# The last two blocks of a four-layer attention kernel cut into parts, under a newly written order of all work

## The chip, the cores and the metric

The kernel runs on one core of a Trainium2 chip. The metric is the device time in microseconds (us) of one execution. The kernel before was timed six times: 332.86 to 335.13 us, median 334.13 us. One more execution was profiled; it took 333.49 us, and its span from the first to the last instruction is 331.8 us. TensorE is called PE here, VectorE DVE, ScalarE ACT, GpSimd POOL; SP is the engine whose queue issues most transfers.

## The reference

x has 2048 tokens of width 512, in bf16. Four layers follow each other, A B A B, each with a residual; both have 32 heads of 16.

```
def _A_ref(x, wqkv, w_phi, wo):                    # linear attention
    q, k, v = split(x @ wqkv)                      # per head
    pq = einsum("bhsd,hdf->bhsf", q, w_phi);  pk likewise
    phi_q = concat([softmax(pq), softmax(-pq)]);  phi_k likewise
    kv = einsum("bhsf,bhsd->bhfd", phi_k, v);  z = einsum("bhsf->bhf", phi_k)
    o = einsum("bhqf,bhfd->bhqd", phi_q, kv) / (einsum("bhqf,bhf->bhq", phi_q, z) + 1e-6)
    return merge_heads(o) @ wo

def _B_ref(x, wqkv, wo):                           # window of 8 keys, 2 apart
    q, k, v = split(x @ wqkv)
    idx = pos[:, None] - 2 * arange(8)
    logits = where(idx >= 0, q . k[idx] / 4, -1e9)
    return merge_heads(softmax(logits) . v[idx]) @ wo

x = x + _A_ref(_layernorm(x), ...)
x = x + _B_ref(_layernorm(x), ...)     # and both once more
```

## The kernel before, in words

The tokens are cut into four blocks of 512, each of four tiles of 128 tokens; x stays in SBUF, as x0 to x3. A stage of the model is one Python function, called for layer pair L (0 or 1) and block b (0 to 3). A function does not issue its work: it puts small steps on named threads, one thread for each stage and engine (`step`). `run` then walks a long written table, `_ORDER`, whose words each name a thread, and issues that thread's next step. Since every engine works through its own instructions in the order in which they were issued, this one table sets the order on PE, DVE, ACT and SP alike. Three more tables belong to it. `_CHOICE` has one digit for each flexible step (`flex`): whether a copy out of PSUM, a normalisation or a residual goes to DVE or to ACT. `_SLOTS` says which buffer each tile takes, in four pools: "big" (8 buffers: the key exponentials Ek, the replicated values Vg, the products prod and pav), "med" (16), "t2" (6) and "ps" (the 8 PSUM banks). A tile that takes a buffer waits until the readers of the one before it are done.

The stages that the change and the prediction speak of:

- Loads (`s_loads`): x0 in four tiles of 128 KB, the raw query and key weights (wraw), the value weights (WA), x1 to x3 in 512 KB each, all on SP's queue. The weights are folded with w_phi on PE before the first projection.
- `s_a1`, keys and values of an A layer: L575 makes the keys of a tile, L581 their exponentials (ACT, +k and -k), L587 the values. On DVE four adds that halve each time (L608 to L621) give the softmax sums, ACT turns them into reciprocals by logarithm and exponential (rr), and L633 multiplies the exponentials of the whole block, 4096 elements a partition. L650 sums keys times values over all tokens, 16 small matmuls a tile, into one PSUM bank for the layer (kvp): nothing that needs the state can start before the last block's L633 and L650.
- `s_a2`: L680 makes queries, L688 their exponentials Eq, L696 (indS) the sums.
- `s_akv`, the change-over from keys to queries: the state is copied (kvT), transposed (L726), and spread into the zero-padded ZM (L735) and R (L739) on DVE.
- `s_a3`: L764 makes the denominators with ZM, DVE and ACT make rho from them. For blocks 0 and 1 PE spreads rho over the heads' rows (L790, bc, into four banks) and DVE multiplies Eq by it from PSUM, tile by tile (L796, mulp). For blocks 2 and 3 rho goes through DRAM instead (Prho, L814). `s_a4` multiplies by the state (L855), and copies oT out of PSUM.
- `s_b1`: the projections of a B layer (L879), copied to QT, K and V. K and V carry 16 tokens of the block before at their front: K's halo is copied on DVE (L905), V's on ACT in two steps (L917, L921, by way of vh). `vrep` then writes V in 32 transfers a block, each 32 partitions high and shifted, into Vg (L931, SP).
- `s_b2`: prod (L960, DVE) multiplies queries by the shifted keys, 4096 elements a partition, one for each of four c; L967 sums over the head (lgt); ACT makes exponentials, PE and ACT the reciprocal sum, DVE the weights PT (L995).
- `s_b3`: pav (L1020, DVE) multiplies PT by Vg, 4096 elements, one for each of four q; L1027 (mo) sums into PSUM, and a copy puts the result into oT.
- `s_out`: for each of four tiles `mm` makes four products that add up over c (L511), one for each q of oT, then the residual: either PE adds x by an identity matmul (L514, "onpe") and ACT copies the result out (L521), or DVE adds x from SBUF (L524). After the last layer two tiles at a time are stored (L535, SP, 256 KB).
- `s_flag`: three small DVE operations count whether the fast path's number ranges were kept, PE sums them over the partitions, three more DVE operations decide. Every engine loads the outcome into a register at the end (L1072) and branches to a general path, which does not run here.

In the last 30 us of the order before, the last four stages of blocks 2 and 3 run beside each other. DVE has the last prod, two pav, PT, six pav in a row, the three counts, a residual of x3, the three deciding operations, three residuals of x3 and three of x2. PE has four sums, the sixteen output products of block 3, the last two sums of block 2 together, and then the sixteen output products of block 2.

## Time and profile before

| | us |
|---|---|
| median of six runs | 334.13 |
| the profiled execution | 333.49 |
| its span | 331.8 |
| PE busy | 311.5 |
| DVE busy | 300.4 |
| ACT busy | 281.4 |
| POOL busy | 5.8 |

Busy time counts an engine's instructions without idle time; matmuls are pipelined and their ends are modelled, so PE's figure says that PE had work, not that it was at its peak. Streams of 512-column matmuls follow each other at 0.22 us (0.86 us for four), although each is shown with 380 ns. The transfers of Vg land 4.8 us after their issue (median), the stores of 256 KB 4.1 us, the first loads of x (128 KB) 4.2 us. POOL has 32 instructions in all, and nearly all of them fill a tile with a constant. The granted clock of PE is full until some 310 us, and 0.83 to 0.87 after that.

### The profile page before, as it was taken

To read this page: it belongs to the slowest core of one execution; us is meant where nothing else is said; L and a number is where in the kernel's file an instruction comes from. 1 tells how busy PE (TensorE), PEld (TensorE's weight loads), DVE (VectorE), ACT (ScalarE), POOL (GpSimd) and SP (SyncE) were. 2 spreads that over 40 slices of the span, in tenths; PEclk is the share of its full clock that TensorE was granted. 3 is DMA by queue.
4 is the path that set the end of the run, shared out by engine and by line. 5 is a ranking of instruction groups with operands and counts; after the bars stand their busy time and mean duration, and the time that the engine had idled before them with its cause. 6 is when DMAs were issued, how large, how long until landed. Compare 5 with 4: busy or idle time off the path is not lost.

```text
span 331.8 us, 7975 instructions
## 1 busy us (share of the span) xinstructions
PE 311.5 (94%) x3189; PEld 149.9 (45%) x3189; DVE 300.4 (91%) x422; ACT 281.4 (85%) x644; POOL 5.8 (2%) x32
## 2 busy tenths in 40 slices
PE   8999997999999999999999999789999999997792
PEld 4545446445444444443444455534444444443231
DVE  5899995898899899999999999498999999999983
ACT  4999995999998898999999999688899997685630
POOL 4000000000000000000000000000000000000000
PEclk9999999999999999999999999999999999999988
DMA  7980000014499889785990200022469988789905
GB/s 208 330 226 3 0 0 4 4 35 103 97 158 140 154 136 164 128 136 117 143 129 14 54 0 2 6 56 90 115 109 144 126 155 174 131 142 155 209 5 168
DMA packets 37325, 35.42 MB, mean 107 GB/s; under 512 B 22944, under 2 KB 32160, under 8 KB 37280
## 3 DMA queue, kind: packets, MB, share of 16 engines
q1 hardware_dynamic: 36752, 34.81, 55.6%
q8 instruction: 27, 0.44, 0.6%
q14 instruction: 18, 0.15, 0.2%
q10 hardware_dynamic: 528, 0.02, 0.1%
HBM read 10.50 MB, written 2.36 MB: 39 GB/s over the span
## 4 chain that ended last, share of the span: by engine, by line
PE 65%; DVE 13%; ACT 11%; DMA 5%; issue 3%; SPq 1%; DVEq 0%; ACTq 0%
PE ps L879 19%; PE ps L511 13%; PE ps L575 6%; PE ps L587 6%; PE ps L680 5%; DMA xnT<-xn 4%; PE ps L967 3%; DVE Eq L796 3%; PE ps L1027 3%; DVE prod L960 3%; ACT oT L186 2%; DVE Ek L633 2%; ACT sqd L531 2%; PE ps L453 2%; PE ps L650 2%
## 5 line engine op out<-in xcount | busy, mean ns | idle before, releaser
L879 PE MATMUL ps<-xnT,WB 128*128 128x512 bf16 x384 | 88.5, 380 | 1.0 <-ACT V L186 0.7
L960 DVE TENSOR_TENSOR prod<-QT,K 128x4096 bf16<-128x4096 bf16 x32 | 72.2, 2287 | 1.1 <-ACT K L186 0.9
L1020 DVE TENSOR_TENSOR pav<-PT,Vg 128x4096 bf16<-128x4096 bf16 x32 | 71.7, 2287 | 0.9 <-PE ps L967 0.4
L879 PEld LDWEIGHTS <-WB 128*128 128x128 bf16 x384 | 42.2, 115 | 44.7 <-issue 7.4
L511 PEld LDWEIGHTS <-oT 128*128 128x128 bf16 x256 | 24.1, 99 | 32.9 <-ACT oT L186 4.0
L186 ACT CAST oT<-ps 128x512 bf16<-128x512 f32 x57 | 31.4, 603 | 7.7 <-PE ps L1027 6.6
L688 ACT ACTIVATE Eq<-ps 128x512 bf16<-128x512 f32 x64 | 35.0, 613 | 1.2 <-PE ps L680 1.1
L581 ACT ACTIVATE Ek<-ps 128x512 bf16<-128x512 f32 x64 | 34.2, 626 | 0.0
L511 PE MATMUL ps<-WoA,oT 128*128 128x512 bf16 x128 | 31.2, 380 | 1.4 <-ACT oT L186 1.4
L511 PE MATMUL ps<-WoB,oT 128*128 128x512 bf16 x128 | 32.5, 389 | 0.0
L680 PE MATMUL ps<-xnT,WA 128*128 128x512 bf16 x128 | 31.0, 380 | 1.0 <-issue 0.8
L587 PE MATMUL ps<-WA,xnT 128*128 128x512 bf16 x128 | 30.7, 379 | 0.0
L575 PE MATMUL ps<-WA,xnT 128*128 128x512 bf16 x128 | 30.0, 379 | 0.4 <-DMA xnT<-xn 0.4
L531 ACT ACTIVATE sqd<-x 128x512 bf16<-128x512 bf16 x48 | 30.0, 635 | 0.3
L524 DVE SCALAR_TENSOR_TENSOR x<-ps,x 128x512 bf16<-128x512 f32 x36 | 23.5, 685 | 1.0 <-PE ps L511 0.8
L521 ACT ACTIVATE x<-ps 128x512 bf16<-128x512 f32 x28 | 16.5, 598 | 8.0 <-PE ps L514 7.6
L439 ACT ACTIVATE xn<-x,nmr,rstd 128x512 bf16<-128x512 bf16 x27 | 21.4, 822 | 2.0 <-DVE nmr L428 2.0
L186 ACT CAST QT<-ps 128x512 bf16<-128x512 f32 x30 | 17.3, 593 | 3.6 <-issue 2.5
L796 DVE TENSOR_TENSOR Eq<-ps,Eq 128x512 bf16<-128x512 f32 x32 | 19.7, 681 | 0.1
L1027 PE MATMUL ps<-pav,indAV 128*32 128x512 bf16 x256 | 17.4, 389 | 2.6 <-DVE pav L1020 2.6
L186 ACT CAST K<-ps 128x512 bf16<-128x512 f32 x30 | 17.7, 596 | 2.1 <-PE ps L879 1.8
L186 ACT CAST V<-ps 128x512 bf16<-128x512 f32 x31 | 17.5, 602 | 2.3 <-PE ps L879 2.3
(126 smaller groups left out, 405.7 us busy)
## 6 DMA issues: line engine op xcount, KB each, us to landing
Vg<-V SPq DMA_DIRECT2D x128, 131.5 KB, 4.8
Prho<-rd SPq DMA_DIRECT2D x8, 512.0 KB
out_dram<-x SPq DMA_DIRECT2D x8, 256.0 KB, 4.1
x<-in_A_x_dram SPq DMA_DIRECT2D x3, 512.0 KB, 6.6
WB<-in_B_wqkv_dram SPq DMA_DIRECT2D x3, 512.0 KB, 11.5
wraw<-in_A_wqkv_dram SPq DMA_DIRECT2D x4, 256.0 KB
x<-in_A_x_dram SPq DMA_DIRECT2D x4, 128.0 KB, 4.2
WA<-in_A_wqkv_dram SPq DMA_DIRECT2D x1, 512.0 KB
```

Source lines behind the costliest of these rows:

```text
L186: self.nc.scalar.copy(out=out, in_=in_)
L511: nc.tensor.matmul(y[:], lhsT=oT[:, c, t * P:(t + 1) * P], rhs=Wo()[:, c, :], start=(c == 0), stop=(c == NB - 1 and not onpe))
L531: nc.scalar.activation(out=sqd[:], in_=xb[:, t, :], func=ACT.Square, accum_out=T["ss"][:, t:t + 1])
L575: nc.tensor.matmul(pk[:], lhsT=xnT[:, t, k, :], rhs=self.WA[:, k, D:2 * D], start=(k == 0), stop=(k == NB - 1))
L581: nc.scalar.activation(out=T["E"][:, t, s, :], in_=T["k", t][:], func=ACT.Exp, scale=1.0 - 2.0 * s)
L587: nc.tensor.matmul(pv[:], lhsT=xnT[:, t, k, :], rhs=self.WA[:, k, 2 * D:3 * D], start=(k == 0), stop=(k == NB - 1))
L680: nc.tensor.matmul(pq[:], lhsT=self.WA[:, k, hb * P:(hb + 1) * P], rhs=xnT[:, :, k, :], start=(k == 0), stop=(k == NB - 1))
L688: nc.scalar.activation(out=self.Eq[L, b][s][:, :, hb, :], in_=T[hb][:].rearrange("p (t i) -> p t i", t=4), func=ACT.Exp, scale=1.0 - 2.0 * s)
L796: nc.vector.tensor_tensor(out=ev, in0=T["pb", s][t][:].rearrange("p (a i) -> p a i", a=NB), in1=ev, op=ALU.mult)
L879: nc.tensor.matmul(pp[:], lhsT=self.WB[:, k, i * D + c:(i + 1) * D:NB], rhs=xnT[:, :, k, :], start=(k == 0), stop=(k == NB - 1))
L960: nc.vector.tensor_tensor(out=pr[:], in0=QT[:, c:c + 1, :].to_broadcast([P, NW, TB]), in1=win, op=ALU.mult)
L1020: nc.vector.tensor_tensor(out=pv[:], in0=PT[:].unsqueeze(1).to_broadcast([P, NB, 2, TB]), in1=vw, op=ALU.mult)
```

## The change

The three tables `_ORDER`, `_CHOICE` and `_SLOTS` are written anew throughout, so every engine's order differs from the first tenth of the work on. Besides:

- For blocks 2 and 3 of the last layer (`split`) the output product of a tile comes in two steps: three of the four products (q = 0, 1, 2) on a thread of their own, which may be issued early, and the fourth with the residual. The last pav, its sums and its copy are cut into two halves of 256 tokens. Each tile is stored for itself.
- In `s_a3` each multiplication by rho is flexible: ACT first copies the PSUM bank to SBUF (bs) and DVE multiplies from there, or DVE reads PSUM as before.
- The key sums of block 3 go in two halves of two tiles in both A layers (`half_k`).
- The halo copies of K and V run on POOL, and POOL's order is now set by the table too.
- The register loads of the flag are issued 12 words of the table after its deciding step, not at the very end (`flag_lag`); on SP this puts the load ahead of the last store. On the other engines it stays last.

```diff
-    "half_k": (),
+    "half_k": ((0, 3), (1, 3)),
+    "split": ((1, 2), (1, 3)),
+    "flag_lag": 12,
...
-_ORDERED = {_E.PE, _E.DVE, _E.Activation, _E.SP}
+_ORDERED = {_E.PE, _E.DVE, _E.Activation, _E.SP, _E.Pool}
...
-        def mm(t, onpe):
+        def mm(t, onpe, cs=range(NB)):
             oT = self.oT[key, b]
-            T[t] = y = self.ps()
-            for c in range(NB):
+            if cs[0] == 0:
+                T[t] = self.ps()
+            y = T[t]
+            for c in cs:
                 nc.tensor.matmul(y[:], lhsT=oT[:, c, t * P:(t + 1) * P], rhs=Wo()[:, c, :],
                                  start=(c == 0), stop=(c == NB - 1 and not onpe))
-            if onpe:
+            if onpe and cs[-1] == NB - 1:
...
+        split = last and (1, b) in _OPT["split"]
+        if split:
+            for t in range(4):
+                add(st + "p", "PE", mm, t, False, range(NB - 1))
         for t in range(4):
-            add(st, "PE", mm, t, _CHOICE[self.nflex] == "1")
+            if split:
+                add(st, "PE", mm, t, _CHOICE[self.nflex] == "1", range(NB - 1, NB))
...
+            elif last and split:
+                add(st, "SP", store, t, t + 1)
...
+        def bev(s, t, direct):
+            if direct:
+                self.slot("t2")
+            else:
+                T["bs", s, t] = self.t2([TB], "bs")
+                nc.scalar.copy(out=T["bs", s, t][:], in_=T["pb", s][t][:])
...
-            nc.vector.tensor_copy(out=self.K[L, b][:, :, 0:16], in_=self.K[L, b - 1][:, :, TB:KVW])
+            nc.gpsimd.tensor_copy(out=self.K[L, b][:, :, 0:16], in_=self.K[L, b - 1][:, :, TB:KVW])
...
-            nc.scalar.copy(out=T["V"][:, :, 0:16], in_=self.vh[L, b - 1][:])
+            nc.gpsimd.tensor_copy(out=T["V"][:, :, 0:16], in_=self.vh[L, b - 1][:])
...
-            nc.scalar.copy(out=self.vh[L, b][:], in_=T["V"][:, :, TB:KVW])
+            nc.gpsimd.tensor_copy(out=self.vh[L, b][:], in_=T["V"][:, :, TB:KVW])
...
         for q in range(NB):
-            add(st, "DVE", pav, q)
-            add(st, "PE", mo, q)
-            self.flex(st, ev, q)
+            m = 2 if q == NB - 1 and (L, b) in _OPT["split"] else 1
+            for i in range(m):
+                a = (i * TB // m, TB // m)
+                add(st, "DVE", pav, q, *a)
+                add(st, "PE", mo, q, *a)
+                self.flex(st, ev, q, *a)
```

How the instructions of the two kernels stand against each other, counted over the whole program:

| instruction | before | after |
|---|---|---|
| DVE, Eq times rho from PSUM / from SBUF | 32 / 0 | 21 / 11 |
| ACT, rho from PSUM to SBUF (bs) | 0 | 11 |
| DVE, residual with sums / of the last layer | 29 / 7 | 34 / 4 |
| PE, identity product of a residual (and its ACT copy) | 28 | 26 |
| xn on DVE / on ACT | 37 / 27 | 44 / 20 |
| DVE, copies of oT, of the rest (QT, K, V, WA, kvT, vaug) | 7, 16 | 11, 12 |
| halo copies on DVE / ACT / POOL | 6 / 12 / 0 | 0 / 0 / 18 |
| L633 over 4096 / over 2048 elements | 8 / 0 | 6 / 4 |
| pav over 4096 / over 8 x 256 | 32 / 0 | 30 / 4 |
| output stores of 256 KB / of 128 KB | 8 / 0 | 4 / 8 |

The order at the places that matter here. At the start SP issues all four tiles of x0 before the first weights (three before, and the fourth later), and the value weights after x1 to x3 (after x1 in before); DVE makes the mask constants before its first statistics, and PE's first projections are twelve query products and sixteen key products, then values (in before keys, then values). At the change-over of each layer the last L650 that waits for DVE has 32 matmuls (64 or 80 in one piece in before); query products stand between the last L650, the transposes and the denominators in the first layer, and the 32 indS products of one block in the second. In the tail DVE has the last prod, two pav, PT, and then block 3's four pav (the last in halves) and block 2's last three (the last in halves), the counts, two residuals of x2, the deciding operations and two more. Block 3's four residuals are on PE and ACT. PE's output products of blocks 3 and 2 stand in pieces of three to six between the sums; the fourth tile of each block has its four products together, after the last half of the sums. On SP a store of two tiles of block 1, which waits for ACT, stands between the fourth and fifth of the last eight Vg loads.

## The prediction

> **What bounds the kernel now.** First the page: busy shares, then busy time by stretch, to see which engine has room in which stage.
>
> ```profile
> PE 311.5 (94%) x3189; PEld 149.9 (45%) x3189; DVE 300.4 (91%) x422; ACT 281.4 (85%) x644; POOL 5.8 (2%) x32
> ```
>
> ```profile
> 89.20:178.20 89.00, 88.16 (x604) 38.98 (x606) 86.77 (x84) 83.88 (x201) 1.31 (x4) 1.00 0.85 135
> 178.20:211.30 33.10, 32.08 (x481) 17.48 (x477) 28.67 (x49) 30.97 (x69) 0.00 (x0) 1.00 0.09 18
> 211.30:319.70 108.40, 100.44 (x980) 45.96 (x976) 104.67 (x117) 86.00 (x205) 0.15 (x1) 0.98 0.70 124
> 319.70:331.80 12.10, 6.18 (x40) 2.25 (x38) 5.03 (x15) 1.67 (x3) 0.00 (x0) 0.87 0.34 115
> ```
>
> The columns after the length are busy PE, weight loads, DVE, ACT, POOL, clock, DMA. In the first B layer (89 to 178) DVE is idle 2.2 us of 89.0, in the second (211 to 320) 3.7 of 108.4: DVE work added there is paid almost in full. Between them, at the change-over from keys to queries, PE and ACT are the full ones. The last 12.1 us hold little of anything. Next the waits of DVE in the second half, and the chain that ended last:
>
> ```profile
> DVE ZM L735 <- PE ps L726: 3.3, 1, 3.3
> ```
>
> ```profile
> 312.96 2.29 DVE pav L1020
> 315.25 0.04 issue
> 315.30 1.05 PE ps L1027 x7
> 316.34 4.62 PE ps L511 x16
> 320.96 0.98 PE ps L1027 x16
> 322.05 2.75 PE ps L511 x12
> 325.02 0.88 PE ps L511 x4
> 325.92 0.69 DVE x L524
> ```
>
> One change-over wait costs DVE 3.3 us in one piece. In the tail the last value product (pav) begins at 317.4 and ends at T = 319.65; its sums (L1027) start only at 320.89, behind sixteen output products of the other block; all sixteen products of the last block follow; the last residual ends at 326.61, so 6.96 us after T. The store is issued then and the span ends at 331.8, 5.2 us later. Prices, from the groups by line:
>
> ```profile
> L796 DVE TENSOR_TENSOR Eq<-ps,Eq 128x512 bf16<-128x512 f32 x32 | 19.7, 681 | 0.1
> L616 DVE TENSOR_TENSOR s<-s 128x512 bf16<-128x512 bf16 x8 | 3.4, 424 | 0.2
> L596 POOL MEMSET vaug<- 128x64 bf16 x8 | 2.8, 486 | 112.4 <-PE ps L511 64.0 <-PE ps L680 45.3 <-DVE prod L960 3.0
> L905 DVE COPY K<-K 128x64 bf16<-128x64 bf16 x6 | 1.1, 176 | 0.0
> L909 POOL MEMSET K<- 128x64 bf16 x2 | 0.3, 152 | 26.6 <-PE ps L855 26.6
> ```
>
> **What the Trainium skill says.** "VectorE: DVE Perf Modes", section The perf-mode tier table: a tensor-tensor operation on bf16 in SBUF runs at 2x, one with a PSUM operand at 1x. The trace agrees: 681 ns from PSUM, 424 ns for the same 512 elements from SBUF. "SBUF — State Buffer", section Who interferes with whom: a DVE instruction with two SBUF inputs contends with a GpSimd instruction that reads SBUF, and whichever starts first holds the ports for its whole length. Nothing here shows it: POOL only fills tiles during the work of before, and the change gives it 18 copies that read. "DMA: Bandwidth & Descriptors", section Anatomy of one DMA: most of a small transfer is a fixed cost, the wait for the write's receipt. The trace agrees: stores of 256 KB land in 3.8 to 4.3 us, loads of 128 KB in 4.2 (median).
>
> **The change, part by part.** The sum is made against the profiled execution (span 331.8, its own time 333.49; the median of the six runs is 334.13, 0.6 above it).
>
> Tail. The last pav comes in halves, and three quarters of most tiles' output product need only the three earlier q. After T, DVE has: three flag counts (0.28 past T in before), two residual tiles at a 0.62 pitch (L524), the three deciding instructions (322.09 to 322.63, 0.54), and two more residuals, 0.62 + 0.69. That is 3.4 us. PE's side runs beside it: eight half-width sums (about 0.5 with latency), one half cast (about 0.4; the full one is 0.60), then a last product and the four fused ones of the last tile (0.87 + 0.2), residual 0.69: some 3.1. I take 3.7, with 0.3 for waits between engines. Gain 6.96 - 3.7 = 3.3. Bounds: 2 (the clock at 0.87 and PE late) to 4. The last store is 128 KB instead of 256: nothing. SP's load of the flag (492 ns, after the last store in before) now stands ahead of the last store; the flag is ready two residuals before that store's data, 1.3 us, so it is hidden; without that cover it costs 0.5.
>
> A store moved in SP's queue: the first half of block 1 is stored between the fourth and fifth of the last eight Vg loads. It waits for two ACT residuals of block 1. From the pav before the last PT: 0.5 (sums) + 1.15 (two casts) + 2.3 (eight products, two identities) + 0.6 is 4.6 us, then 0.42 for the issue, 2.9 for four loads at 0.73, 4.8 to land: 12.7. The split pav that reads them stands 0.6 + 6 x 2.2 = 13.8 behind the same point. Hidden with 1.1 to spare; if landing takes 6.8 it costs 0.9.
>
> DVE work up to T. Eleven of 32 rho products read an SBUF copy: 11 x 0.257 = -2.8. Six K halos go to POOL: -1.1. Five more residuals with sums, 0.70 each from start to start: +3.5. Seven more xn at 0.33 (three take 1.06): +2.3. One more xnT copy: +0.6. The other casts from PSUM change places but not number. Halves of the last key block in both layers: each of five instructions costs about 0.15 more, less what overlaps: +1.2. Halved pav: +0.15. Sum +3.8; with the overlap of neighbours counted along the two instruction lists I get +3.3. By place: about +1 before the first change-over, +1.6 in the first B layer, -0.5 from there to the second change-over, +1.4 after it. ACT: 11 copies at 0.60 (+6.6), 12 halo copies (-3.1), seven xn (-5.5), two residuals and five accumulator reads (-2.2), the rest about +0.4: some -4 in all, so the copies fit into ACT, idle 22 us from 211 to 320. PE: two identity products fewer, -0.4.
>
> Change-overs. Second: in before, from the end of the last Ek product (208.0) to the zero-padded states (ZM, 211.29) DVE waits 3.3: 64 kv products (1.1), cast 0.6, a 0.95 stop of the PE queue at the indS products ahead of the transposes. With halves only 32 kv follow the last product (0.55), and the indS products stand complete beside the cast: 0.6 + 0.6 + 0.4 + 0.15 = 1.8, a gain of 1.5. First: the last Ek product ends at 51.7 and ZM comes at 56.34, with 1.8 us of DVE work in the gap that now lies elsewhere (the mask constants in the wait for x at the start). The like sum gives 2.0. DVE alone would reach ZM 2.6 earlier; PE has 1.2 less to stream up to the last kv; ACT has some 2 us more before the last Ek, mostly filler. I take 1.6. Against it the start: the fourth tile of x is now issued ahead of the weights on SP, 0.43 to 0.50 for its issue, and PE waits for these weights from 5.94: +0.4. Net 1.2. Bounds 0 to 2.6. Loading the value weights behind all of x lets them land some 3 us later, but the value products now come after twelve query and sixteen key products (28 x 0.22 = 6 us): covered.
>
> POOL copies. Lower bound nothing (each runs while DVE waits or reads PSUM); upper bound 0.49 each, as the strided memset, held against DVE: 18 x 0.49 = 8.8. A plain 64-element memset takes 0.15. I take nothing and keep the upper end as a rival.
>
> Sum: -3.3 (tail) - 1.2 (first change-over and start) - 1.5 (second) + 1.6 - 0.5 + 1.4 (DVE work) = -3.5. From 333.49 that is 330.0; from the median 330.6. I say 330.2.
>
> **The rivals.** A, larger gain: the new order also removes waits in the middle. DVE is idle 5.1 us between 56.3 and 89.2 and the first change-over could give 2.6. Half of the former and all of the latter: -3.5 - 2.5 - 1.4 = -7.4, 326.1. For it: DVE is not the full engine there. Against: PE is busy 31.9 of 32.9 us in that stretch. B, the tail alone: ACT, 98% busy from 20 to 40 us, makes the first change-over no earlier, and the second is eaten by the 1.9 us of DVE work ahead of it: -3.5 + 2.7 = -0.8, 332.7. For it: ACT's and PE's fill there. C, slower: POOL's reading copies take the shared port between two DVE instructions, and the next prod or pav waits. At 0.39 us, the median memset of vaug, all 18 cost 7.0: -3.5 + 7.0, so 337.0. It decides from (3.5 + 1.7) / 18 = 0.29 us a copy. For it: the B layers have DVE back to back, so no copy finds the port free for long. Against: a small copy may be nearer to 0.15, and where DVE waits anyway it costs nothing.
>
> **How the numbers follow.** Half a per cent, 1.7 us, is about what a measurement of this kernel can tell from no change: faster is below 332.5, slower above 335.8. Forecast 0.48 (327.5 to 332.5), A 0.20, B 0.17, C 0.15. Faster: nearly all of the forecast's, all of A, four tenths of B, some 0.72; same 0.13; slower 0.15. The range goes from 325.5 (A with a little more) to 334.8 and leaves out C and the end of A.
>
> **What would show it.** From the end of the last pav half to the last residual 3 to 4 us, and to the end of the span some 9 instead of 12.15. The wait of ZM for the transposes below 2 us in the second layer. DVE busy 301 to 302 in all. Rho products from SBUF at 0.42. POOL copies at 0.15 to 0.25, and prod and pav still at 2.29 without holes before them. Wrong if prod or pav last 2.5 or more, or start late, beside POOL copies (C); if DVE waits for Vg before the last pav halves (the moved store); or if ZM is not earlier than 56.3 and 211.3 (B).

## The result, and the profile after

The changed kernel takes 332.79 us (median of 34 runs, 330.5 to 334.4), the kernel before 334.23 us (71 runs, 332.4 to 336.93). The ratio is 0.9945, 95% interval 0.993 to 0.996. So 1.4 us by the medians, 1.8 by the ratio, where 3.9 were forecast (334.13 to 330.2): the sign is right, the size more than twice too large. The profiled execution took 332.49 us, its span is 330.7.

The page's first row after, to be read against the row of before:

```profile
PE 310.8 (94%) x3203; PEld 149.5 (45%) x3203; DVE 302.5 (91%) x443; ACT 279.5 (85%) x634; POOL 26.8 (8%) x50
```

DVE has gained 2.1 us and ACT lost 1.9. The prediction's list of instructions had +3.3 to +3.8 for DVE and some -4 for ACT: the directions are right, the sizes about half. POOL stands at 26.8 instead of 5.8, for 18 more instructions.

The same execution by stage. The columns after the length are busy PE, weight loads, DVE, ACT, POOL, clock, DMA share and GB/s; the cuts are the first ZM, the first prod, the last pav of the first B layer, ZM of the second layer, the last pav (T in the prediction), the last residual, the end.

```profile
0.00:54.40 54.40, 51.80 (x593) 28.54 (x594) 48.38 (x105) 46.98 (x98) 5.19 (x30) 1.00 0.43 117
54.40:86.69 32.29, 31.59 (x503) 15.67 (x502) 27.45 (x68) 31.21 (x75) 0.15 (x1) 1.00 0.17 44
86.69:179.61 92.92, 90.54 (x652) 40.77 (x650) 88.91 (x88) 84.18 (x199) 7.95 (x10) 1.00 0.78 132
179.61:210.94 31.33, 30.90 (x457) 16.58 (x457) 28.17 (x50) 29.58 (x67) 0.00 (x0) 1.00 0.10 19
210.94:321.25 110.31, 102.79 (x982) 46.76 (x983) 106.28 (x125) 86.91 (x199) 13.53 (x9) 1.00 0.68 121
321.25:325.14 3.89, 3.17 (x22) 1.18 (x20) 3.28 (x12) 0.61 (x2) 0.00 (x0) 1.00 0.72 252
325.14:330.70 5.56, 0.00 (x0) 0.00 (x0) 0.01 (x1) 0.00 (x0) 0.00 (x0) 0.83 0.29 83
```

Before, the same cuts lie at 56.34, 89.18, 178.25, 211.29, 319.65, 326.61 and 331.80. The first prod comes 2.5 us earlier; the last pav of the first B layer 1.4 later; the second ZM 0.35 earlier; T, which was to be slightly earlier, 1.6 later; then the end wins. So in this pair of executions the gain of the first change-over is given back in the next 93 us, and that of the second change-over in the 110 us after it.

The waits of DVE from 205 us to the end of the last pav (total, times, longest), which answer to the 3.3 us shown of before:

```profile
DVE ZM L749 <- PE ps L740: 1.8, 1, 1.8
DVE x L529 <- PE ps L516: 1.3, 2, 1.0
```

1.8 is the very figure that the prediction worked out for the second change-over. And the tail, in the chain of waits:

```profile
319.19 1.10 ACT oT L189 x2
320.29 0.05 issue
320.34 0.39 PE ps L516
320.73 0.33 PE ps L1045 x8
321.06 1.18 PE ps L516 x5
322.25 0.01 PE ps L1079
322.25 0.33 PE ps L1045 x8
322.58 1.85 PE ps L516 x8
324.43 0.02 issue
324.45 0.69 DVE x L529
```

Where before sixteen output products (L511, here L516) kept PE from the sums of the last pav until 1.2 us after T, eight half-width sums now run at 320.7, the other half's at 322.25, and only eight products remain behind them. From T to the last residual 3.89 us, forecast 3.7: DVE's own list is as long as was forecast, and it waits once, 0.46 us, for PE. Yet the last residual ends at 325.14 against 326.61: 1.5 us, not 3.3.

**One execution or several.** Two more profiles of the kernel before were taken (e11 and e15), and three experiments below leave nearly everything up to T as it is (e2 puts the last pieces together again, e4 moves only the flag's load, e9 one load of Vg). So each stretch is known from three executions of the old order and four of the new:

| stretch, us | before | after | difference of means | forecast |
|---|---|---|---|---|
| start to first prod | 89.2, 90.7, 89.8 | 86.7, 86.4, 86.2, 86.1 | -3.5 | |
| first prod to last pav, layer 0 | 89.1, 89.2, 89.2 | 92.9, 92.6, 94.0, 93.7 | +4.2 | |
| the two together | 178.3, 179.9, 178.9 | 179.6, 179.0, 180.2, 179.8 | +0.6 | +0.4 |
| to second ZM | 33.0, 32.8, 32.8 | 31.3 (all four) | -1.5 | -2.0 |
| to the last pav | 108.4, 108.3, 108.3 | 110.3, 110.2, 110.1, 110.2 | +1.9 | +1.4 |
| to the last residual | 7.0, 5.6, 5.6 | 3.9 (without e2) | -2.2, or -1.7 without the 7.0 | -3.3 |
| to the end | 5.2, 5.4, 5.0 | 5.5, 5.5 (changed kernel, e9) | +0.3 | 0 |

Without the 7.0 the differences add up to -0.4 us, with it to -0.9: less than the measured 1.4 to 1.8. Spans of single executions scatter by 1 us; the clock, under e11 and e15 below, accounts for most of the rest. The largest difference from the forecast is the tail.

### The profile page after: what moved, and what is told of

Same layout as the page of the kernel before. It is cut to its first block, busy times and chain, and to the rows that moved or that the text cites. A ratio compares the mean times of both kernels' runs of the same rounds, so it can differ in the third digit from the quotient of the medians.

```text
span 330.7 us, 8061 instructions
## 1 busy us (share of the span) xinstructions
PE 310.8 (94%) x3203; PEld 149.5 (45%) x3203; DVE 302.5 (91%) x443; ACT 279.5 (85%) x634; POOL 26.8 (8%) x50
## 4 chain that ended last, share of the span: by engine, by line
PE 62%; ACT 13%; DMA 11%; DVE 8%; SPq 3%; issue 2%; ACTq 0%; DVEq 0%
PE ps L893 19%; PE ps L516 10%; DMA Vg<-V 7%; PE ps L601 6%; PE ps L589 6%; PE ps L694 5%; PE ps L981 3%; ACT Ek L595 3%; ACT Eq L702 3%; DMA xnT<-xn 3%; PE ps L1045 2%; SPq L945 2%; DVE Eq L812 2%; PE ps L456 2%; ACT sqd L536 2%
## 5 line engine op out<-in xcount | busy, mean ns | idle before, releaser
L1036 DVE TENSOR_TENSOR pav<-PT,Vg 128x4096 bf16<-128x4096 bf16 (+1 forms) x34 | 71.8, 2163 | 1.9 <-DMA Vg<-V 1.2
L516 PEld LDWEIGHTS <-oT 128*128 128x128 bf16 x256 | 23.6, 98 | 34.4 <-ACT oT L189 4.3
L189 ACT CAST oT<-ps 128x512 bf16<-128x512 f32 (+1 forms) x55 | 29.5, 584 | 8.1 <-PE ps L1045 7.7
L516 PE MATMUL ps<-WoB,oT 128*128 128x512 bf16 x128 | 32.8, 380 | 0.3
L516 PE MATMUL ps<-WoA,oT 128*128 128x512 bf16 x128 | 30.9, 380 | 1.6 <-DVE x L529 1.4
L694 PE MATMUL ps<-xnT,WA 128*128 128x512 bf16 x128 | 31.3, 380 | 0.2 <-DVE Eq L812 0.2
L529 DVE SCALAR_TENSOR_TENSOR x<-ps,x 128x512 bf16<-128x512 f32 x38 | 24.9, 685 | 2.2 <-PE ps L516 2.1
L189 ACT CAST K<-ps 128x512 bf16<-128x512 f32 x32 | 18.7, 590 | 3.6 <-PE ps L893 3.5
L1045 PE MATMUL ps<-pav,indAV 128*32 128x512 bf16 (+1 forms) x272 | 17.6, 370 | 3.3 <-DVE pav L1036 2.9
L935 POOL COPY vh<-V 128x64 bf16<-128x64 bf16 x6 | 7.4, 1234 | 161.9 <-ACT V L189 161.9
L526 ACT ACTIVATE x<-ps 128x512 bf16<-128x512 f32 x26 | 15.1, 593 | 6.1 <-PE ps L519 5.6
L189 ACT CAST QT<-ps 128x512 bf16<-128x512 f32 x31 | 18.2, 600 | 2.3 <-PE ps L893 2.3
L601 PEld LDWEIGHTS <-xnT 128*128 128x128 bf16 x128 | 12.3, 98 | 14.7 <-issue 0.4
```

The costliest lines, as they stand in the source:

```text
L189: self.nc.scalar.copy(out=out, in_=in_)
L516: nc.tensor.matmul(y[:], lhsT=oT[:, c, t * P:(t + 1) * P], rhs=Wo()[:, c, :], start=(c == 0), stop=(c == NB - 1 and not onpe))
L529: nc.vector.scalar_tensor_tensor(out=xb[:, t, :], in0=T[t][:], scalar=1.0, in1=xb[:, t, :], op0=ALU.mult, op1=ALU.add, **kw)
L601: nc.tensor.matmul(pv[:], lhsT=xnT[:, t, k, :], rhs=self.WA[:, k, 2 * D:3 * D], start=(k == 0), stop=(k == NB - 1))
L694: nc.tensor.matmul(pq[:], lhsT=self.WA[:, k, hb * P:(hb + 1) * P], rhs=xnT[:, :, k, :], start=(k == 0), stop=(k == NB - 1))
L1036: nc.vector.tensor_tensor(out=pv, in0=PT[:, :, lo:lo + n].unsqueeze(1).to_broadcast([P, NB, 2, n]), in1=vw, op=ALU.mult)
```

## The experiments

All start from the changed kernel unless said otherwise. Ratios are to the kernel before; the changed kernel itself stands at 0.9945 (0.993 to 0.996), so 0.003 is one microsecond.

**e1 and e6: the V halo copies on ACT or DVE.** The first theory was that POOL's copies give the gain back: they last 0.23 us where DVE leaves them alone and up to 3.44 where it does not, and a Vg load stood behind one of them before DVE's only wait for Vg.

```diff
-            nc.gpsimd.tensor_copy(out=T["V"][:, :, 0:16], in_=self.vh[L, b - 1][:])
+            nc.scalar.copy(out=T["V"][:, :, 0:16], in_=self.vh[L, b - 1][:])          # e1; e6: nc.vector.tensor_copy
-            nc.gpsimd.tensor_copy(out=self.vh[L, b][:], in_=T["V"][:, :, TB:KVW])
+            nc.scalar.copy(out=self.vh[L, b][:], in_=T["V"][:, :, TB:KVW])            # e1; e6: nc.vector.tensor_copy
```

> The changed kernel with its twelve V halo copies (into vh and out of it) on ACT at the same places of the order; the six K halos stay on POOL. Theory (a POOL copy that is held up behind DVE delays one Vg load, and DVE loses 1.2 us before a pav of the first B layer, which is most of what is missing at the second change-over): DVE's wait for Vg (1.2 us) is gone, ZM of the second layer comes at 209.5 to 210.1 instead of 210.94, and the kernel is 0.8 to 1.4 us faster than the changed one: ratio to before 0.990 to 0.992. Rival (PE and ACT bound the stretch up to the second change-over, so the wait costs nothing): the wait is gone but ZM stays at 210.7 to 211.3 and the time within 0.4 us of the changed kernel, 0.994 to 0.996; ACT's 3 us more could even make it slower.

> The changed kernel with its twelve V halo copies on DVE, the K halos left on POOL. Theory (as for the fills): the waits for Vg and Prho go, DVE pays 12 x 0.15 = 1.8 us, so within 0.8 us of the changed kernel, ratio to before 0.993 to 0.998. Rival 1 (no hold-up matters): 1.8 us slower, 0.999 to 1.001. Rival 2 (as on ACT, an engine with a long queue brings the copy later than POOL does): waits for Vg grow to several us, ratio 1.003 or more.

Measured: e1 1.013 (1.0089 to 1.0171), e6 1.0215 (1.0175 to 1.0255): 6 and 9 us slower than the changed kernel. Both expectations of the theory missed; only the second rival of e6 had it. The first copy to vh starts at 104.0 us in e1 and 105.1 in e6, against 95.9 on POOL, and DVE waits for Vg 4.4 and 4.1 us in all instead of 1.2. The copy costs 0.25 us on ACT and 0.17 to 0.18 on DVE; that it waits its turn in a queue of other work is what the later Vg loads point to. Part of the loss can be PE's clock, which fell to half for 3.41 us in both profiled executions (at 317.1 in e1, at 113.7 in e6), in or just behind pauses of PE of 2.9 and 3.9 us. So these two say nothing against POOL's copies; they show what POOL's own queue is worth under this order.

**e5: no halo copies at all.**

```diff
-            nc.gpsimd.tensor_copy(out=T["V"][:, :, 0:16], in_=self.vh[L, b - 1][:])
+            nc.gpsimd.memset(T["V"][:, :, 0:16], 0.0)
...
-            nc.gpsimd.tensor_copy(out=self.vh[L, b][:], in_=T["V"][:, :, TB:KVW])
+            pass
...
-            nc.gpsimd.tensor_copy(out=self.K[L, b][:, :, 0:16], in_=self.K[L, b - 1][:, :, TB:KVW])
+            nc.gpsimd.memset(self.K[L, b][:, :, 0:16], 0.0)
```

> The changed kernel with each of its twelve halo copies into K and V replaced by a fill with zeros, on POOL at the same place of the order, and the six copies out to vh left out: the halo of three blocks in four is not computed. A fill reads nothing. Theory (a POOL copy that reads SBUF waits behind DVE, so SP's queue is held and the Vg and Prho loads behind it land late): POOL busy falls from 26.8 to 12 us or less, DVE's waits for Vg and Prho vanish (1.2 us in the changed kernel's profile, 3.3 in that with the flag load at the end), the first B layer (first prod to last pav of layer 0) takes 91.0 to 91.8 us instead of 92.6 to 94.0, ratio to before 0.989 to 0.992. Rival (the wait is taken up behind it by PE, which is full there, or the transfers are late for other reasons): 92.3 us or more, ratio 0.993 to 0.996.

Measured: 0.990 (0.9864 to 0.9937), 1.5 us (0.2 to 2.8) faster. But the stretch that was to shrink did not: first prod to last pav 92.5 us. POOL is busy 7.5 us, and DVE still waits for Vg in it:

```profile
DVE pav L1035 <- DMA Vg<-V: 1.3, 1, 1.3
```

The ratio lies where the theory had it, but by another way: the wait was not for a copy on POOL. What the copies cost beside fills is 0.2 to 2.8 us, and this experiment cannot place it.

**e9: the load that DVE waits for.** SP's queue shows where the wait comes from. In the new order, from the transposes of block 3 on:

```profile
117.98 2.05 SPq L447 DMA_TRANSPOSE xnT<-xn  x1
120.07 20.25 SPq L945 DMA_DIRECT2D Vg<-V  x24
```

and before, with the run of loads ahead of them:

```profile
107.63 11.06 SPq L931 DMA_DIRECT2D Vg<-V  x16
122.11 1.78 SPq L444 DMA_TRANSPOSE xnT<-xn  x1
124.01 17.50 SPq L931 DMA_DIRECT2D Vg<-V  x20
```

A block's V goes out in sixteen transfers (128 for the eight blocks in the list of DMA issues), not in 32 as the description above has it. Behind the transposes of block 3 stand twelve transfers of block 0 in the new order, eight in the old; the chain of waits has the last of the twelve land 8.47 us after its issue, where 4.7 is the median. e9 moves four of them ahead (SP's order, stage and step):

```diff
   b1_01v/3
+  b1_00v/1
   a4_03o/0        # the transposes
-  b1_00v/1
   b1_00v/2
   b1_00v/3
```

> The changed kernel with the second Vg load of block 0, first layer (four transfers), moved in SP's queue from behind the xnT transposes of block 3 to just ahead of them, where SP stands idle for 1.9 us. Theory, formed after the fills (which kept the wait of 1.3 us although no copy was left to wait for): twelve transfers of block 0 issued in one run behind those transposes make the last of them land 8.5 us after its issue, and that is the wait. Then with eight in that run the wait before the pav at 135 falls from 1.2 to under 0.4, and the first B layer takes 91.3 to 92.0 instead of 92.5 to 92.9 us, the kernel 0.6 to 1.3 us faster than the changed one, ratio to before 0.990 to 0.993. Rival (DVE's wait there is taken up by PE or ACT behind it): wait gone, time the same, 0.994 to 0.996. Second rival: the transposes come later and with them the products of block 3; slower, 0.997 or more.

Measured: 0.9955 (0.9932 to 0.9978), and the stretch 93.7 us. The wait is gone, as the theory said; the time is the same, as the first rival said. This execution has another wait, for Prho, which the profile of the changed kernel does not show, but which comes and goes from one execution of this order to the next. The wait in e4, whose order is the changed kernel's up to the end of its work:

```profile
DVE Eq L829 <- DMA Prho<-rd: 2.0, 1, 2.0
```

With this wait for Prho the stretch takes 93.4 to 94.2 us (e3, e4, e8, e9, e12, e13, e14), without it 92.5 to 92.9 (the changed kernel, e2, e5, e7 at 92.7). None of the three profiles of before has a wait for Prho or Vg there.

**e16 and e17: the load of Prho moved up.** e16 puts the second Prho load of block 3 ahead of the transposes of block 1; its buffer is that of an ACT square of the weights, which moves some 85 words back in the table. e17 has e9's move as well.

```diff
   a3_03/1         # first Prho load
+  a3_03/2         # second Prho load
-  bound.ACT/0
   a4_01o/0        # the transposes
...
-  a3_03/2
...
+  bound.ACT/0
   bound.ACT/1
```

> The changed kernel with the second Prho load of block 3, first layer, ahead of the xnT transposes of block 1 in SP's queue instead of behind them, and the square of WA on ACT, whose buffer it takes, moved from there to just ahead of its fellow some 25 us later. Theory (in the first B layer it is transfers that come late, not an engine's work: eight of eleven profiles of the new order have a wait of 1.9 to 2.2 us for this load, and the three cuts of work moved nothing): the wait is gone, first prod to last pav 91.5 to 92.7 instead of 93.6 to 94.2, 0.6 to 1.6 us faster than the changed kernel, ratio to before 0.990 to 0.993. Rival (another wait takes its place): 93 us or more, 0.994 to 0.997.

> Both moves of loads together (the second Prho load of block 3 and the second Vg load of block 0 ahead of the transposes they stood behind). Theory (transfers): DVE waits for neither, first prod to last pav 90.8 to 91.8, 1.2 to 2.5 us faster than the changed kernel, ratio to before 0.987 to 0.991. Rival (an engine or the chain of one block sets the stretch after all): 92.5 or more, ratio 0.993 to 0.997.

Measured: 1.0153 (1.0108 to 1.0198) and 1.0124 (1.0083 to 1.0166), 6 to 7 us slower than the changed kernel; both sides of both expectations missed. SP's queue in e17:

```profile
84.22 1.56 SPq L825 DMA_DIRECT2D Prho<-rd  x2
85.95 6.90 SPq L447 DMA_TRANSPOSE xnT<-xn  x1
94.22 14.51 SPq L945 DMA_DIRECT2D Vg<-V  x8
```

In the changed kernel the transposes begin at 85.65 and take 4.71. Behind 512 KB more they take 6.90, and so the projections of block 1, which read them, come late. From 86.5 to 110 us, first in the changed kernel, then in e17 (busy PE, weight loads, DVE, ACT, POOL, then the clock):

```profile
86.50:110.00 23.50, 22.60 (x149) 10.64 (x151) 22.20 (x30) 20.27 (x41) 4.59 (x7) 1.00 0.82 153
86.50:110.00 23.50, 19.29 (x106) 8.62 (x107) 16.91 (x22) 13.77 (x31) 2.90 (x4) 0.85 0.75 107
```

ACT waits 4.1 us at once for a K product, and DVE 6.3 us at once for ACT's rstd. PE pauses for 4.2 us (4.8 in e16), and its clock is at half for 6.8 us, of which 4.9 lie behind the pause (5.9 in e16); this costs PE up to 2.5 us more (3.0 in e16; estimates, half of that time). So the loss has two parts, the late transposes and the slower clock that came with the pause, and the runs do not part them. The load of Prho was late because the transposes went first; in this order putting it first costs more than its wait did.

**e12, e13, e14, e18: work taken out of one engine, then of all three.** If neither POOL nor the two loads hold the first B layer, an engine's work might.

```diff
-            for k in range(NB):                                                # e12, and stop=(k == nk - 1)
+            nk = NB - 1 if L == 0 and b in (1, 2) and i == 1 else NB
+            for k in range(nk):
...
+                w = D // 2 if key == "B0" and b >= 2 else D                    # e13: DVE residual over 0:w
...
+            w = D // 2 if key == "B0" and b >= 2 else D                        # e14: ACT square over 0:w
```

> The changed kernel with eight matmuls of the K projections of blocks 1 and 2 in the first B layer left out (the last quarter of their contraction isn't computed): PE 8 x 0.215 = 1.7 us less in that stretch, nothing else changed. Theory now (PE's work, 90.5 of 92.9 us, sets the end of the first B layer, so DVE's waits there cost nothing and what the earlier first prod gained is given back as PE work): first prod to last pav 90.9 to 91.5 against 92.6 to 94.0, ratio to before 0.989 to 0.991. Rival (DVE sets it, as the prediction had it): 92.4 or more, ratio 0.993 to 0.996.

> The changed kernel with the seven DVE residuals of blocks 2 and 3 in the first layer over half their columns (the other half of x isn't updated): DVE 7 x 0.26 = 1.8 us less in the first B layer. Theory (PE sets it): 92.3 us or more, ratio to before 0.993 to 0.996. Rival (DVE sets it): 90.8 to 91.5, ratio 0.989 to 0.991.

> The changed kernel with the eight squares of blocks 2 and 3 in the first layer over half their columns (half of the variance sum is left out): ACT 8 x 0.25 = 2.0 us less in the first B layer. Theory (PE sets it): 92.3 us or more, 0.993 to 0.996. Rival (ACT's queue sets it, as the slow kernels with more work on ACT suggest): 90.5 to 91.5, ratio 0.988 to 0.991.

> The three cuts of before (eight K matmuls, half of seven DVE residuals, half of eight ACT squares, all in the first B layer, not computed) in one kernel. Theory (three engines, each 90 to 97% busy there, bind by turns, so that one alone gives nothing): together they take 1.2 to 2.0 us off that stretch, first prod to last pav 91.6 to 92.6 beside 93.6 to 94.2, ratio to before 0.988 to 0.991. Rival (the transfers for the next block set it): 93.4 or more, ratio 0.992 to 0.996.

| | ratio, 95% interval | first prod to last pav |
|---|---|---|
| e12, PE 1.7 us less | 0.9949 (0.9927 to 0.9972) | 94.0 |
| e13, DVE 1.8 us less | 0.9926 (0.9902 to 0.9949) | 93.6 |
| e14, ACT 2.0 us less | 0.9932 (0.9912 to 0.9952) | 94.2 |
| e18, all three | 0.9916 (0.9883 to 0.9948) | 91.7 |

No single cut shortens the stretch, against 93.4 to 94.2 for executions with the wait for Prho (all three have it, 2.0 to 2.2). The three together do: 91.7, with 0.3 of that wait left, so 0.8 to 1.2 below the 92.5 to 92.9 of the executions without it. That is for 5.5 us of work. e12's theory, that PE sets the end there, falls; so does DVE alone. That the three bind by turns, with transfers in between, fits this, but it is not shown: each length is from one execution, and by the times e18 is 1.0 us (-0.2 to 2.2) faster than the changed kernel, which is not clear of nothing.

**e8 and e10: work moved from DVE to ACT.** The prediction priced added DVE work at its own length. Its reverse, four residuals of block 2 in the second layer (e8) and five xn in the first B layer (e10), given to ACT:

```diff
 _CHOICE: digits 321 to 324 (residuals of a4_12o)             0000 -> 1111    # e8
 _CHOICE: digits 97, 98, 177, 188, 189 (xn, b3_00o, b3_02o, a4_03o)  1 -> 0   # e10
```

> The changed kernel with four residuals of block 2 in the second layer's first half (behind the A output product) on PE and ACT instead of DVE: an identity product and an ACT cast each. Theory (DVE sets the second B stage, as the prediction counts it): DVE 4 x 0.69 less, PE 4 x 0.22 and ACT 4 x 0.6 more; ZM to the last pav 107.8 to 109 instead of 110.1 to 110.3, 1 to 2.5 us faster than the changed kernel, ratio to before 0.987 to 0.992. Rival (PE is as full as DVE there): 110 to 111.5, ratio 0.994 to 0.999.

> The changed kernel with five of the nine xn of the first B layer's blocks (two of block 0 and three of block 2) on ACT instead of DVE. Theory of the prediction (DVE work added in the first B layer is paid almost in full): DVE 5 x 0.33 = 1.65 us less, first prod to last pav 91.0 to 91.8, 0.8 to 1.6 us faster than the changed kernel, ratio to before 0.989 to 0.992. Rival, after the four residuals (ACT's queue is what DVE waits for there, 5 x 0.6 us are added to it): no gain or slower, 0.995 to 1.003, with more waits of DVE for ACT.

(Of e10's five, two belong to block 0, one to block 2 and two to block 3; the expectation names them otherwise.) Measured: e8 1.0067 (1.0046 to 1.0088), the second B stage 114.5 us instead of 110.2; e10 1.012 (1.0075 to 1.0166), the first 99.5. In e8 DVE does 2.4 us less, and waits:

```profile
DVE q L545 <- ACT sqd L533: 3.9, 2, 3.3
DVE prod L971 <- ACT K L186: 1.4, 2, 1.1
DVE q L543 <- ACT x L523: 1.4, 1, 1.4
```

With 2.3 us more work on ACT, in a queue where the sums for the next normalisation stand behind it, the kernel is 4 us slower. Not all of this need be ACT's queue: PE has four more products, and in both profiled executions its clock fell to half for 3.41 us inside the stretch (at 248.0 in e8, at 155.4 in e10, there behind a pause of PE of 2.9 us). The nine of e8's eighteen executions with a mean clock of 0.996 or more take 335.75 us (median), still some 3 us more than the changed kernel. So the residuals and xn that the new order adds to DVE are not to be read as a loss of so many microseconds: on ACT, in this order, they cost more. ACT's share of 79% in the second B stage did not show that.

**e7: rho read from PSUM throughout.**

```diff
-                direct = _CHOICE[self.nflex] == "1"
+                direct = True
```

> The changed kernel with all 32 rho products reading PSUM, the eleven ACT copies to SBUF left out. Theory (the prediction's term of -2.8 us of DVE work holds, all of it on the path): first prod about 1.0 us later and the second B stage (ZM to the last pav) about 1.8 longer, 2 to 3 us slower than the changed kernel, ratio to before 1.000 to 1.004. Rival (PE or ACT set the pace where these products stand, early in each B stage, so the 2.8 bought little): under 1 us slower or even faster, as ACT has 6.6 us less; ratio 0.992 to 0.997.

Measured: 0.9983 (0.9966 to 1.0), 1.3 us (0.5 to 2.0) slower than the changed kernel. DVE is busy 305.1 us instead of 302.5, so the 2.8 of the prediction is nearly right as work (682 ns from PSUM, 416 from SBUF in the changed kernel); half of it is on the path. The first prod comes at 87.4 us (86.1 to 86.7 in the four executions above), and the second B stage takes 111.3 instead of 110.2. Between the theory's 2 to 3 and the rival's 1.

**e3: the key sums of block 3 in one piece.**

```diff
+            if m == 2:      # the first half's steps do nothing; the second half's run over all four tiles
+                ...
```

> The changed kernel with the last key block of each layer in one piece: the five sums and the product over all four tiles at the places of the second half, the kv products of all four tiles behind them. Theory (the halves are worth 1.5 us at each change-over): DVE's wait before ZM in the second layer 2.3 to 3.3 instead of 1.8, and the product itself 2.29 instead of 1.23 at the end of the chain; 1 to 2.5 us slower than the changed kernel, ratio to before 0.997 to 1.002. Rival (ACT's exponentials set the change-over and the halves only add fixed costs on DVE): the wait grows but ZM comes at the same time, 0.994 to 0.996 or lower.

Measured: 0.9995 (0.9981 to 1.0009), 1.7 us (1.0 to 2.4) slower than the changed kernel, as the theory had it. The waits of DVE from the first B layer's last pav to 214 us:

```profile
DVE ZM L770 <- PE ps L761: 2.3, 1, 2.3
DVE s L635 <- ACT rk L642: 1.1, 1, 1.1
```

From the last pav to ZM the second change-over takes 32.85 us, against 31.33 in four executions with halves and 32.8 to 33.0 before: 1.5 us, all of that stretch's gain. At the first one ZM comes at 54.55 against 53.8 to 54.4. That is 0.5 above the mean of the four, but e12, whose cut comes later, has 54.8: a worth of the halves there can't be told from scatter. Most of the 2.7 us by which ZM is earlier (54.1 against 56.8 in the mean) comes from the rest of the order.

**e2, e4: the tail and the flag.**

```diff
-                add(st + "p", "PE", mm, t, False, range(NB - 1))                  # e2
+                add(st + "p", "PE", lambda t: T.__setitem__(t, self.ps()), t)
-                add(st, "PE", mm, t, _CHOICE[self.nflex] == "1", range(NB - 1, NB))
+                add(st, "PE", mm, t, _CHOICE[self.nflex] == "1")
...
-                a = (i * TB // m, TB // m)
+                a = (0, TB)            # and nothing for i = 1
...
-    "flag_lag": 12,                                                              # e4
+    "flag_lag": 1000,
```

> The changed kernel with the tail in one piece again: the last pav, its sums and its cast whole for both of the last blocks, and each tile's output product as one group of four at the place of its last part; stores still per tile. Theory (the tail's parts are worth 3.1 us): from the last pav's end to the last residual about 6 to 7 us instead of 3.9, the kernel 2.5 to 3.5 us slower than the changed one, ratio to before 1.001 to 1.006. Rival (most of the gain comes from what the new order puts ahead of the tail, not from the parts): 4 to 5 us, ratio 0.996 to 0.999.

> The changed kernel with SP's load of the flag behind the last store, as before the change. Theory (hidden, as the prediction has it): the time within 0.3 us of the changed kernel, ratio to before 0.994 to 0.996. Rival (the load holds SP just ahead of the last store and is the 0.37 us by which the end became longer): last residual to end 5.2 instead of 5.56, 0.3 to 0.5 us faster. A second rival: now the load stands at the end, after the store's landing or beside it, and costs up to 0.6.

Measured: e2 0.9996 (0.9976 to 1.0016), 1.7 us (0.9 to 2.5) slower than the changed kernel, 6.3 us from T to the last residual. By the times this is between theory and rival, 1.7 us for the parts and not 3.1. Its DVE waits at the place that the parts were made for:

```profile
323.51 0.69 DVE L529 SCALAR_TENSOR_TENSOR x<-ps,x 128x512 bf16<-128x512 f32 x1 [2.64 <-PE ps L516]
```

But the 6.3 us are not a length at full clock. In the 8 us ahead of T this execution's clock is 0.79, the third figure from the right:

```profile
312.50:320.50 8.00, 6.33 (x31) 2.37 (x36) 8.00 (x5) 2.87 (x5) 0.00 (x0) 0.79 0.21 49
```

PE waits for two pav in a row there. The second wait, before and in e2:

```profile
315.30 1.05 PE L1027 MATMUL ps<-pav,indAV 128*32 128x512 bf16 x8 [1.58 <-DVE pav L1020]
```

```profile
313.94 1.04 PE L1045 MATMUL ps<-pav,indAV 128*32 128x512 bf16 x8 [1.59 <-DVE pav L1036]
```

In the changed kernel the first wait, 0.80 us, is the only one:

```profile
312.36 0.61 PE L1045 MATMUL ps<-pav,indAV 128*32 128x512 bf16 x8 [0.80 <-DVE pav L1036]
```

There the pieces of the output products fill the second. In e2 the clock was at half from 313.49 to 316.90, in the second pause and behind it. That held PE back by up to 1.5 us (an estimate: half of the 2.96 us that lie behind the pause), so at full clock the tail of e2 would take 4.8 to 6.3 us, and the parts are worth between 0.9 and 2.4. The times point to the low side: of e2's 22 executions the twelve with a mean clock of 0.996 or more have a median of 332.85 us, the other ten 334.35; e4, which was timed beside it and differs from the changed kernel only in the flag's load, has 332.55. What the parts save would then be for the most part the pause and the slow clock that can follow it.

e4: 0.9952 (0.9937 to 0.9968), the same as the changed kernel. The flag's load is hidden where it is, and is not what makes the end 0.3 us longer.

**e11 and e15: the kernel before, twice more.**

> The kernel before, profiled once more. Theory: its stretches repeat within 0.3 us except where a transfer decides (first prod to last pav 89.0 to 89.7, ZM of the second layer to the last pav 108.2 to 108.6, last pav to last residual 6.9 to 7.0, from there to the end 5.1 to 5.5), so the differences between the two kernels by stretch are not chance. Rival: the first B layer of before was a lucky execution, 90 us or more here.

> The kernel before, a third profile, for the tail alone. The two profiles so far have 6.96 us (clock 0.79 in the 8 us ahead of the last pav's end) and 5.58 us (clock 1.00) from the last pav to the last residual. Theory (the prediction read its tail from an execution whose clock had just dipped): 5.4 to 5.8 where the clock is 1.00 there, 6.5 or more only where it is below 0.9. Rival (the length has nothing to do with the clock): 6.5 or more at 1.00.

e11 beside the other runs of the same kernel gives 0.999 (0.9969 to 1.0012). The two B stages repeat within 0.2 us in all three profiles; the tail, expected at 6.9 to 7.0, does not. The profiled execution of before from which the prediction was made, in the 8 us ahead of T and from T to the last residual:

```profile
311.65:319.65 8.00, 5.43 (x39) 1.62 (x28) 8.00 (x5) 4.27 (x9) 0.00 (x0) 0.79 0.46 121
319.65:326.61 6.96, 6.24 (x41) 2.25 (x38) 5.08 (x15) 1.67 (x3) 0.00 (x0) 1.00 0.33 109
```

and e11:

```profile
313.02:321.02 8.00, 5.43 (x48) 1.76 (x40) 8.00 (x5) 4.28 (x9) 0.00 (x0) 1.00 0.46 121
321.02:326.60 5.58, 4.86 (x34) 1.74 (x26) 5.08 (x15) 1.67 (x3) 0.00 (x0) 1.00 0.40 136
```

The column before the last two is the granted clock: 0.79 in the first stretch of the first execution, 1.00 in that of the second. The chain of waits of e11 shows where the time sits:

```profile
317.28 3.67 PE ps L511 x16
320.95 0.98 PE ps L1027 x16
321.93 0.11 PE ps L1057
322.04 2.75 PE ps L511 x12
```

Sixteen products of the other block take 3.67 us here and 3.51 for fifteen in e15; in the prediction's profile 4.62. All that follows in the tail is the same to a hundredth (0.98, 2.75). In e15 the clock is 1.00 as well and T to the last residual 5.59. So the theory holds in all three: 5.6 us at full clock, 7.0 where it dipped.

**The clock of all executions.** The dip is no rarity of one execution. Every execution on record has its mean granted clock; a dip of 3.41 us at half lowers it by 0.005 (what else is missing to 1.000 is at the end, where PE has no work left), as 0.990 in the prediction's execution against 0.996 and 0.995 in e11 and e15. Of 232 executions of the kernel before (e11, e15 and those timed beside the experiments) 120 have 0.992 or less; of 36 of the changed kernel none has, nor of the 44 of e4 and e9; the lowest is 0.993. The 43 of before at 0.995 or more take 333.0 us in the mean, the 120 334.6; the changed kernel takes 332.6 in the mean. So where the clock holds the two kernels are some 0.4 us apart, as the stretches at full clock say too, and most of the measured gain goes with clock that the old order loses and the new one keeps. This is a relation over executions, not an experiment: where in the kernel the other executions of before dip isn't recorded.

## Why the prediction was wrong, by its own steps

**The tail, the step that failed.** "[T]he last residual ends at 326.61, so 6.96 us after T" was read from an execution whose clock had dipped to 0.79 just before T; two others have 5.6. The mechanism was right, and the 3.7 worked out for after measured 3.89. But the term "6.96 - 3.7 = 3.3" was mis-sized: at full clock it is 1.7 (5.6 - 3.9). This is 1.6 of the 3.1 us by which the stretches at full clock fall short of the forecast; 0.5 each are in the stretch up to the second ZM and in the second B stage, and the rest in the start with the first B layer and in the end. It could have been seen: sixteen products at 4.62 us are 0.29 each, the twelve after them, in the lines that the prediction shows, 0.23. The prediction allowed for the clock only in the tail after, as a bound on its own 3.7, and from a figure that doesn't belong there: in its execution the clock was full from 318.46 to 328.70 us, and the 0.87 of the last stretch is what came after PE's last product at 325.9. What it had no term for is that the old order loses clock in many of its executions and the new one does not; this made the measured gain larger than the stretches at full clock give. In this part the gain was luck. (Its items for PE's side of the tail add up to 2.7, not 3.1; DVE's list is the longer one either way.)

**The change-overs.** The second is right to a tenth: DVE's wait fell from 3.3 to 1.8, and without the halves the 1.5 us of the stretch are gone (e3). The further 0.5 booked up to it did not appear in that stretch. The first was worth more (2.7 at ZM, forecast 1.2 net), and mostly for another reason than the halves, whose part there can't be told from scatter. What gives the rest was not tried.

**DVE work in the B layers.** As work the prediction has two figures that don't agree: its list gives +3.3, its signs "301 to 302", which is +0.6 to +1.6; measured are 302.5, +2.1. As a price it was incomplete. First B layer: +1.6 forecast, +4.2 measured, of which DVE's busy time is 2.1 in the profiled pair and the rest waits, for transfers above all. Second: +1.4 forecast, +1.9 measured. The premise, that DVE work there is paid almost in full, is not what e7, e8, e10 and e13 show: 2.6 us more on DVE cost 1.3 (e7), 1.8 less gave 0.6 where it was simply left out (not clear of nothing), and there was a loss where ACT took it. Up to the end of the first B layer the two errors cancel, by luck: +0.6 measured, +0.4 forecast. That the earlier first prod gains nothing because three engines and the transfers take turns in holding what follows is made likely by e12 to e14 and e18, not shown; which of them holds it in which microsecond stays open, as does how much of the +4.2 the wait for Prho makes (about 1.2 of it between executions that have it and those that don't).

**The POOL copies.** "I take nothing", the prediction said, with rival C at 7 us. prod and pav last 2.29 us as before (2.32 at most), so POOL's copies don't make DVE's instructions longer, and e5 leaves 0.2 to 2.8 us for them in all: C falls. The copies themselves were expected at 0.15 to 0.25 us; eleven of the eighteen took longer, up to 3.44, also beyond the 0.49 that the prediction named as upper bound.

**The moved store and the flag.** No pav waits for Vg in the last 30 us, and e4 shows the flag's load hidden. The end behind the last residual is 0.3 us longer in the mean, forecast nothing. It is not the flag, and it may be scatter: other profiled executions of the new order have 5.1 to 5.8 us there.

**The rivals.** B's time, 332.7, is nearly the measured one, but not by its reason: the second change-over was not eaten by the work ahead of it. And it is a gain of 0.8 us counted from 333.49, the single profiled execution, about half of what was measured. A and C are out.

## What to carry to other kernels

Before a stretch is taken as a gain, look at the granted clock in and just ahead of it, and divide a run of equal matmuls by their number: a length read from one execution can hold a dip that the next one lacks, and the same question goes to every experiment that comes out slow. The dips seen here stand at pauses of PE, so a change that fills or opens such a pause can move time beyond it: the dip in the prediction's execution cost 1.4 us. In a stretch where three engines are 90% busy or more, the length of an instruction is no price for moving it: taking 1.8 us from one engine gave nothing that could be measured, and the kernel that gave 2.3 us to an in-order queue with late work behind it was 4 us slower. And a load that is late because another went first may be late for a good reason; look at who reads the other.

## What was not expected of the hardware

**PE's clock behind short pauses.** Ahead of PE's last product the clock is either full or half in the twenty traces. Eight have a stretch at half, 3.41 us long, or 6.83 in e16 and e17. Each begins in a pause of PE or within 0.5 us of its end: in the execution of before after 0.99 us and in 1.58 us of pause, in e2 after 0.80 and in 1.59, in e1, e6, e10, e16 and e17 at pauses of 2.9, 3.9, 2.9, 4.8 and 4.2 us, in e8 behind one of 0.81. But pauses don't always bring it: e11 and e15 have the same 0.98 or 0.99 and 1.58 us as the execution of before, and keep the full clock. What decides is not shown.

**Small copies on POOL.** A copy of 64 elements a partition on POOL takes 0.23 us alone and up to 3.44 us beside DVE. POOL and DVE at the same time in the changed kernel:

```profile
249.01 3.44 POOL L935 COPY vh<-V 128x64 bf16<-128x64 bf16 x1 [120.72 <-ACT V L189]
252.40 0.23 POOL L919 COPY K<-K 128x64 bf16<-128x64 bf16 x1
252.57 0.23 POOL L931 COPY V<-vh 128x64 bf16<-128x64 bf16 x1
```

```profile
245.67 6.68 DVE L974 TENSOR_TENSOR prod<-QT,K 128x4096 bf16<-128x4096 bf16 x3
252.28 0.68 DVE L529 SCALAR_TENSOR_TENSOR x<-ps,x 128x512 bf16<-128x512 f32 x1
```

The long copy ends at 252.45, just after the three prod in a row, each with two SBUF operands, have ended; the two that run beside a residual from PSUM take 0.23. The Trainium skill, "SBUF — State Buffer", section Who interferes with whom, names such contention, with whichever comes first holding the ports. Here the small copy is recorded as the longer one, beyond the length of one prod (2.28 us), and DVE's instructions were not measurably longer; a fill on POOL, which reads nothing, takes 0.15 us at the same places in e5 (0.35 at most).
